# Residual added by an accumulating DMA, and an absolute value by a bit mask, in a gated linear attention followed by a GEGLU layer

## The chip, the cores and the metric

The kernel runs on one core of one Trainium2 chip. The metric is the device time of one execution in microseconds (us). Five engines matter: TensorE (PE: matrix products; its weight loads are listed as PEld), VectorE (DVE), ScalarE (ACT), GpSimd (POOL) and SyncE (SP). DMAs are issued from the queues of SP and of POOL. Each engine works through its own instructions in order; an instruction that waits holds up all behind it on that engine.

## What is computed

Two stages. The first is a linear attention with complex decay over batch 4, 8 heads, 768 steps and head size 48; the second is a GEGLU layer with a gated residual over 3072 tokens of width 384 and an inner width of 1536. In the reference, cut to what matters:

```
scale = min(|a|, 0.999) / (|a| + 1e-6)
S_t   = (a_t * scale) * S_{t-1} + k_t v_t^T        (complex a; S starts at 0)
y_t   = q_t . Re(S_t)
x     = y, all heads side by side: 3072 x 384
g, val = x @ w_gate, x @ w_val
out   = x + sigmoid(x @ w_res) * ((gelu(g) * val) @ w_out)
```

All inputs and the output are float32. The kernel keeps x and the operands of the large products in bfloat16.

## The kernel before, in words

The sequence of each batch is cut into three groups of 256 steps, each of two chunks (c = 0, 1) of 128 steps, so there are 12 groups. The groups are put into seven units: unit 0 has one group, units 1 to 5 have two, unit 6 has one. A chunk of 128 tokens is also the block in which the second stage makes its output.

For each group, phase angles and decay magnitudes come from `a_re` and `a_im`:

- `p1_steps` (lines 179 to 200): logarithm of the magnitude and the ratio that becomes the angle, ACT and DVE in turn (L189, L197 and L198 on DVE); `p1_arctan` makes the angle.
- `cs_l` sums the logarithms within a chunk on PE (L212); `ex` takes the exponentials E and Ei on ACT.
- `cs_t` (L229) sums the angles on PE (L236, L238; L224 and L226 prepare what is carried over from earlier groups) and reduces them to a fraction of a turn on DVE: L243 makes the rounded value r, L244 the difference fg. When the second chunk is done, L246 writes the absolute value of fg beside it, for both chunks at once.
- `p2_sin` (L249) takes two sines on ACT, of the absolute fraction and of the fraction itself: the cosine and sine of the angle, CS.
- `products` multiplies q and k with E and Ei (L309, L314) and with CS (L321). `attention` does the rest: transposes (L346, L349), scores (L356) and their mask (L359), chunk states (L386), and the output y (L394, L396), which ACT writes to the tile x (L399) in bfloat16. The state carried from group to group is G (L370 to L375).
- G needs a decay factor M per row. From unit 3 on M is made from values that lie along a row and must be turned into a column. `turn` (L258 to L267) does this by DMAs on POOL's queue: L262 writes one or two rows (dm) to DRAM, L265 reads them back (m) turned, twice for the two halves. `decay3` multiplies the results on DVE (L282, L283).

The second stage, for each unit: `xt_step` transposes x (L424; copies L428 on ACT and L430 on DVE), `gv_step` makes the gate and value products (L439, L443), Gelu on ACT and their product on DVE (L446), `rp_step` the residual gate (L455), and `op_step` the out-projection of one block (L463). `op_step` then multiplies by the gate on DVE (L466), adds x (L467), and SP stores the block (L469).

The main loop calls `phase_x(u)` and `phase_y(u)` in turn. `phase_x(u)` weaves together the out-projections of unit u - 1, the second half of unit u's attention, the sums, exponentials and sines of unit u + 1, and `p1_steps` and `p1_arctan` of unit u + 2. `phase_y(u)` weaves the gate and value products of unit u, the products of unit u + 1 and the first half of its attention. `weave` gives each step a place between 0 and 1, and the steps are recorded in that order; a scheduler that knows the dependences then sets the order on each engine. ACT's function tables are loaded in a fixed order (logarithm and exponential, then sine, then Gelu), so Gelu work of `phase_y` follows the sines of `phase_x`.

POOL's queue carries, besides the transfers of `turn`, the loads of v (L150) and of the weights, and one-element copies (L171) that hold back the v loads until the k of the same group has landed. SP's queue carries the loads of a, q and k and the stores of the output.

Pools: two buffers for the output block ot, ten for x, four PSUM buffers shared by most products.

## Time and profile before

| what | value |
|---|---|
| median of 8 runs | 329.46 us (326.8 to 331.75) |
| the profiled execution | 327.09 us |
| its span, first to last instruction | 325.3 us |
| TensorE clock granted, mean | 0.946 |
| L246, DVE, 12 times | 947 ns each |
| L467, DVE, 24 times | 550 ns each |
| L466, DVE, 24 times | 546 ns each |
| L198, DVE, 12 times (one input, 128x768 float32) | 555 ns each |
| stores of the output L469, 24 times, 192 KB | 2.2 us from issue to landing |
| v loads on POOL L150, 24 times | 895 ns each to issue |
| L262 and L265 on POOL, 15 and 20 times | 0.51 and 0.70 us each to issue |

How to read it: a group row names line, engine, operation, written and read tiles, shape and count, then busy time and the mean of one in ns, then idle time of the engine before it and what ended that. A row of waits names who waited for whom, the total in us, how often, and the longest. A row of the timeline has start, duration, engine, line, operation and tiles, and in brackets the idle time before it. A row of stretches has start and end, the length, then the busy time of PE, PEld, DVE, ACT and POOL with the number of instructions, then the granted clock as a share, the share of the DMA engines' time and GB/s. A DVE instruction in a timeline can start a little before the one ahead of it ends.

### The profile page before, as it was taken

Reading aid. Unit: us, or ns where it says so; the run is one execution under the profiler, and the core shown is the slowest. Engines: PE = TensorE matmul, PEld = TensorE weight load, DVE = VectorE, ACT = ScalarE, POOL = GpSimd, SP = SyncE. Lnnn points to the kernel's source line nnn. Section 1 sums busy time; section 2 is a strip of 40 time slices with the busy share of each in tenths; the row PEclk is TensorE's granted clock in tenths of the full one; section 3 lists DMA queues with packets and bytes.
Section 4 is the critical chain, followed back from the end, with each engine's and each line's share of the span. In section 5 each row is a group of like instructions: output and inputs, shape, how many; then the busy total and the mean of one; then the engine's idle time right before and its main releaser. Section 6 shows DMA issues by size and latency. Waiting matters only on the chain. (4 is left out here: it accounts for less than half of the span.)

```text
span 325.3 us, 5797 instructions
## 1 busy us (share of the span) xinstructions
PE 269.4 (83%) x2175; PEld 169.9 (52%) x2200; DVE 248.9 (77%) x453; ACT 209.1 (64%) x353; POOL 57.9 (18%) x93
## 2 busy tenths in 40 slices
PE   0337927799876999778997989998989999899995
PEld 0116624577433666444664546564555665455682
DVE  2456768988499995699992999984999948974463
ACT  4539684556997557967468956568765582756150
POOL 1207413022061220243030360000400002000000
PEclk9955676979999999999999999999999999999999
DMA  8999999989999894476360480000110002100101
GB/s 168 204 193 186 167 180 164 189 159 186 195 174 192 182 92 57 78 169 73 70 53 2 89 108 26 0 2 3 50 50 2 2 0 51 48 2 0 71 29 48
DMA packets 134587, 30.23 MB, mean 93 GB/s; under 512 B 126496, under 2 KB 134560, under 8 KB 134560
## 3 DMA queue, kind: packets, MB, share of 16 engines
q1 hardware_dynamic: 103296, 23.60, 36.3%
q0 software_dynamic: 31264, 6.27, 22.7%
q8 instruction: 17, 0.28, 0.3%
q14 instruction: 10, 0.08, 0.1%
HBM read 31.31 MB, written 4.74 MB: 111 GB/s over the span
## 5 line engine op out<-in xcount | busy, mean ns | idle before, releaser
L439 PE MATMUL gp<-xT,wg 128*128 128x512 bf16 (+1 forms) x236 | 62.6, 348 | 7.1 <-DVE xT L430 3.6
L124 ACT ACTIVATE h<-gp 128x512 bf16<-128x512 f32 (+1 forms) x84 | 44.4, 536 | 33.0 <-PE gp L439 30.5
L443 PE MATMUL vp<-xT,wv 128*128 128x512 bf16 (+1 forms) x243 | 62.2, 349 | 0.3
L446 DVE SCALAR_TENSOR_TENSOR h<-h,vp 128x512 bf16<-128x512 bf16 (+1 forms) x84 | 49.6, 603 | 11.9 <-PE vp L443 8.0
L463 PE MATMUL op<-wo,h 128*128 128x384 bf16 x288 | 50.2, 326 | 7.8 <-ACT Ei L124 5.9
L463 PEld LDWEIGHTS <-h 128*128 128x128 bf16 x288 | 27.8, 98 | 28.4 <-issue 11.0
L351 ACT COPY qk<-tp 96x512 bf16<-96x512 bf16 x48 | 27.9, 580 | 21.5 <-PE tp L349 12.9
L359 DVE TENSOR_TENSOR atm<-at,mask 128x512 bf16<-128x512 f32 x48 | 32.9, 685 | 7.2 <-PE at L356 7.0
L439 PEld LDWEIGHTS <-wg 128*128 128x128 bf16 x252 | 23.3, 98 | 20.3 <-issue 8.1
L443 PEld LDWEIGHTS <-wv 128*128 128x128 bf16 x252 | 23.7, 98 | 15.1
L189 DVE TENSOR_TENSOR ai<-s,ai 128x768 f32<-128x768 f32 x12 | 11.1, 955 | 23.7 <-ACT s L124 23.7
L124 ACT ACTIVATE CS<-fg,hpi 128x768 bf16<-128x768 f32 x12 | 11.2, 935 | 26.0 <-DVE fg L246 26.0
L474 ACT ACT_TABLE_LOAD x21 | 26.9, 1283 | 1.1 <-PEq L612 0.7
L346 PE MATMUL tp<-ident,Q 128*96 128x128 bf16 x192 | 19.9, 229 | 7.1 <-DVE Q L321 6.4
L346 PEld LDWEIGHTS <-Q 128*96 128x96 bf16 x192 | 17.0, 129 | 14.8 <-DVE Q L321 9.9
L349 PE MATMUL tp<-ident,K 128*96 128x128 bf16 x192 | 22.1, 234 | 0.0
L150 POOL DMA_DIRECT2D v<-in_v_dram x24 | 21.4, 895 | 3.3 <-DMA v<-in_v_dram 1.3
L236 PE MATMUL cst<-ai,lt0b 128*128 128x384 f32 x24 | 11.5, 565 | 11.8 <-ACT ai L124 11.0
L352 DVE COPY qk<-tp 96x512 bf16<-96x512 bf16 x48 | 19.8, 413 | 1.7 <-ACT qk L351 1.4
L212 PE MATMUL csl<-ar,lt0a 128*128 128x384 f32 x24 | 11.4, 559 | 10.8 <-DMA ar<-in_a_re_dram 10.8
L356 PE MATMUL at<-qk 96*128 96x128 bf16 x192 | 19.7, 226 | 0.1
L394 PEld LDWEIGHTS <-atm 128*128 128x128 bf16 x192 | 12.7, 97 | 13.2 <-DVE atm L359 11.7
(84 smaller groups left out, 514.7 us busy)
## 6 DMA issues: line engine op xcount, KB each, us to landing
ar<-in_a_re_dram SPq DMA_DIRECT2D x24, 192.0 KB, 4.5
ai<-in_a_im_dram SPq DMA_DIRECT2D x24, 192.0 KB, 4.2
q<-in_q_dram SPq DMA_DIRECT2D x24, 192.0 KB, 3.8
k<-in_k_dram SPq DMA_DIRECT2D x24, 192.0 KB, 3.8
out_dram<-ot SPq DMA_DIRECT2D x24, 192.0 KB, 2.2
v<-in_v_dram POOLq DMA_DIRECT2D x24, 96.0 KB, 5.2
wg<-in_moe_w_gate_dram POOLq DMA_DIRECT2D x4, 288.0 KB, 11.3
wv<-in_moe_w_val_dram POOLq DMA_DIRECT2D x4, 288.0 KB, 12.6
```

What stands on the lines that cost most here:

```text
L124: tab(nc.scalar.activation(**kw))
L150: nc.gpsimd.dma_start(out=t[:, c], in_=rows(v, g, c))
L346: nc.tensor.transpose(out=tp[0:DD, j * 128:j * 128 + 128], in_=Q(x), identity=ident)
L349: nc.tensor.transpose(out=tp[0:DD, 512 + j * 128:640 + j * 128], in_=K(x), identity=ident)
L351: nc.scalar.copy(out=qk[0:DD, 0:512], in_=tp[0:DD, 0:512])
L352: nc.vector.tensor_copy(out=qk[0:DD, 512:1024], in_=tp[0:DD, 512:1024])
L359: nc.vector.tensor_tensor(out=atm, in0=at, in1=mask4, op=OP.mult)
L439: nc.tensor.matmul(out=gp, lhsT=wg[:, fi, ffi * 128:(ffi + 1) * 128], rhs=xT[:, fi, :], start=(fi == 0), stop=(fi == KD - 1))
L443: nc.tensor.matmul(out=vp, lhsT=wv[:, fi, ffi * 128:(ffi + 1) * 128], rhs=xT[:, fi, :], start=(fi == 0), stop=(fi == KD - 1))
L446: nc.vector.scalar_tensor_tensor(out=h2[:, ffi, :], in0=h2[:, ffi, :], scalar=0.5, in1=vp, op0=OP.mult, op1=OP.mult)
L463: nc.tensor.matmul(out=ps, lhsT=h2[:, ffi, jj * 128:(jj + 1) * 128], rhs=wo[:, ffi, :], start=(ffi == 0), stop=(ffi == KF - 1))
L474: tab(nc.scalar.preload_act_table_set(nm))
```

## The change

The absolute value in `cs_t` is made by clearing the sign bit of the value read as a 32-bit integer, an operation with one input, where it was the larger of the value and its negative. In `op_step`, for all units but the last, DVE no longer adds x to the block: SP stores the product alone, and POOL's queue then issues a DMA that reads the bfloat16 tile x and adds it to the stored float32 block in DRAM. The dependence between the two is kept by the framework: POOL waits for the store before it issues the second. The blocks of the last unit (two of 24) are made as before.

```diff
         if c == C - 1:
-            nc.vector.scalar_tensor_tensor(out=fg[:, :, 0, :], in0=fg[:, :, 1, :], scalar=-1.0, in1=fg[:, :, 1, :],
-                                           op0=OP.mult, op1=OP.max)
+            nc.vector.tensor_scalar(out=fg[:, :, 0, :].bitcast(mybir.dt.int32), in0=fg[:, :, 1, :].bitcast(mybir.dt.int32),
+                                    scalar1=0x7FFFFFFF, scalar2=None, op0=OP.bitwise_and)
...
         nc.vector.scalar_tensor_tensor(out=ot, in0=T["sg", u][:, jj], scalar=1.0, in1=ps, op0=OP.add, op1=OP.mult)
-        nc.vector.tensor_tensor(out=ot, in0=ot, in1=T["x", token(u, jj)], op=OP.add)
         t0 = token(u, jj) * 128
+        if u == NU - 1:
+            nc.vector.tensor_tensor(out=ot, in0=ot, in1=T["x", token(u, jj)], op=OP.add)
         nc.sync.dma_start(out=out[t0:t0 + 128, :], in_=ot)
+        if u < NU - 1:
+            nc.gpsimd.dma_start(out=out[t0:t0 + 128, :], in_=T["x", token(u, jj)], accum_op=OP.add)
```

In the changed file the accumulating DMA is on line 472, the store on 470 and the remaining addition on 469; the lines up to 466 are where they were.

## Prediction

> **What bounds the kernel now.** I read the share of each engine first, then a table of stretches, then the waits, and last the timelines of VectorE (DVE) and GpSimd (POOL) in one stretch. The profiled execution took 327.09 us; its span is 325.3, so 1.8 us lie around it. It belongs to the faster half of the eight runs (median 329.46). I work in differences and take the sum off the median.

> ```profile
> span 325.3 us, 5797 instructions
> ## 1 busy us (share of the span) xinstructions
> PE 269.4 (83%) x2175; PEld 169.9 (52%) x2200; DVE 248.9 (77%) x453; ACT 209.1 (64%) x353; POOL 57.9 (18%) x93
> ```

> No engine is full. The program alternates between phase_x (decay and angle work, the out-projection) and phase_y (the gate and value matmuls). I cut the span at the ScalarE (ACT) table loads. The next five rows are phase_x of units 1 to 5, which I call S1 to S5; the last row is the phase_y between S3 and S4.

> ```profile
> 83.00:103.60 20.60, 15.21 (x84) 7.80 (x84) 16.29 (x26) 18.53 (x28) 6.94 (x10) 1.00 1.25 184
> 128.40:150.40 22.00, 17.52 (x88) 9.42 (x87) 17.52 (x32) 18.33 (x28) 8.47 (x13) 1.00 0.58 105
> 174.60:196.70 22.10, 18.57 (x92) 10.33 (x92) 17.47 (x34) 18.43 (x29) 8.34 (x13) 1.00 0.51 81
> 221.80:240.60 18.80, 16.54 (x86) 9.41 (x86) 15.04 (x28) 14.79 (x23) 4.78 (x8) 1.00 0.13 34
> 265.60:279.50 13.90, 12.62 (x72) 7.20 (x72) 10.06 (x20) 7.65 (x11) 1.98 (x3) 1.00 0.16 44
> ...
> 196.70:221.80 25.10, 24.44 (x259) 15.44 (x262) 22.70 (x41) 15.25 (x30) 0.00 (x0) 1.00 0.01 1
> ```

> After the length come TensorE (PE), its weight loads, DVE, ACT and POOL. In phase_y PE is busy 24.44 of 25.10 us: PE is the bound there, and a shorter DVE buys next to nothing. In S1 to S5 PE leaves 5.4, 4.5, 3.5, 2.3 and 1.3 us, 17 us together; that is all that this change can win there. Whether DVE holds these stretches is told by the waits:

> ```profile
> ACT CS L124 <- DVE fg L246: 26.0, 12, 5.7
> ...
> DVE M L282 <- DMA m<-dm: 0.9, 1, 0.9
> ```

> Both sines of every group (ACT, 12 pairs) wait for the L246 that the change edits. After the last sine come the Gelu table and phase_y, so phase_y begins when DVE has reached its last L246. The second row matters as much: once DVE waited for the decay factors, which POOL's queue brings. DVE in S4, the start first, then the duration:

> ```profile
> 230.52 0.55 DVE L198 TENSOR_SCALAR ar<-ar 128x768 f32<-128x768 f32 x1
> 230.99 0.55 DVE L467 TENSOR_TENSOR ot<-ot,x 128x384 f32<-128x384 f32 x1
> 231.46 1.08 DVE L243 TENSOR_SCALAR r<-cst 128x384 f32<-128x384 f32 x2
> ...
> 234.25 0.55 DVE L243 TENSOR_SCALAR r<-cst 128x384 f32<-128x384 f32 x1
> 234.75 0.16 DVE L282 TENSOR_TENSOR M<-m 96x8 f32<-96x8 f32 x1
> ...
> 236.63 0.95 DVE L246 SCALAR_TENSOR_TENSOR fg<-fg 128x768 f32<-128x768 f32 x1
> 237.50 0.55 DVE L467 TENSOR_TENSOR ot<-ot,x 128x384 f32<-128x384 f32 x1
> ```

> DVE runs without a break, so what is taken out moves everything behind it. What counts is the distance between starts: 0.47 us for L467 (230.99 to 231.46) and for L198, 0.87 for L246 (236.63 to 237.50).

> POOL in the same stretch; the pair L265 brings the factors that L282 reads at 234.75:

> ```profile
> 229.55 0.48 POOL L262 DMA_DIRECT2D dm<-E  x1 [0.61 <-ACT E L124]
> 230.65 1.50 POOL L265 DMA_DIRECT2D m<-dm  x2 [0.61 <-DMA dm<-Ei]
> 232.14 0.52 POOL L262 DMA_DIRECT2D dm<-ar  x1
> ```

> **The mask.** The twelve L246 become one-input operations of the same 768 elements. Nearest row: L198, also one input, 555 ns against 947 ns. The new one is int32 and steps over 48 of every 96 elements, which no row shows; at worst it costs what L246 costs. [...] So I take L198's pace: 0.87 - 0.47 = 0.40 us each. [...]

> **The residual add.** 22 of 24 L467 go from DVE (22 x 0.47 = 10.3 us of its time); the last two stay, at the end of the program. The store of SP waits for L466 instead, some 1.3 us earlier, with no new queueing in front of it; only its neighbours among the loads shift. In their place POOL gets 22 transfers L472 (96 KB read, 192 KB added in DRAM), each of which waits for its store: 2.2 us median from issue to landing, 1.8 to 4.1. POOL works in order, so all behind it waits too: the v loads, the copies L171, and the decay transfers L262/L265. Issue on POOL: L262 takes 0.51 us for 16 rows and the v loads 0.9 us for 128 x 8 pieces; L472 has 128 rows, nearer the former, so 0.6 (between 0.5 and 0.9). Their time in flight no row shows; a plain store's 2.2 is the lower end, three times that, for reading, adding and writing in turn, the upper; it matters only where a transfer behind it is urgent (S3, S4). Behind the last one lies no work; it is done some 10 us before the end. Tile x is held longer, but its ten buffers come round two units later.

> **Stage by stage**, in the order in which the built program puts the instructions (the scheduler moved some). Savings count up to the last L246.

> - The two stages before S1 hold one and two masks: 0.4 + 0.8. Thereafter PE waits for a chain of ACT work in a part where DMA is 90% busy; between 0 and 1.2, I take half, 0.6.
> - S1: one L467 (0.47), two masks (0.8), one L466 now behind the mask (0.47): 1.7. POOL stands until the store of the first token lands (issued 102.30 behind SP's loads, so about 106); the decay pieces and v loads behind it are needed only from S2 on.
> - S2: three L467 (1.4), two masks (0.8), less an L224 moved ahead and L282 (0.55): 1.65. Its m transfers were issued at 134.3, ahead of the first L472: no new wait.
> - S3: three L467 and two masks: 2.2. But L282 now stands in front of the last L246, and DVE reaches it at 190.04 (before, the L243 in front of it ended its turn at 190.91 + 0.47 = 191.38; less two L467 and one mask, 1.34). Its data come from the second of an L265 pair, issued at 187.26 and 188.13 after the transfers that feed it had come in, as they will again (the L472 ahead of the pair, whose store now goes out at about 181.6, is issued by 185); that transfer takes 3.3 us: 191.5. DVE stands 1.4 us. Left: 0.6.
> - S4: two L467 (0.94), two masks (0.8), less an L224 moved ahead (0.47): 1.25. L282: the L265 pair was issued at 230.65 and 231.40, and landed 3.1 us later by the median, the second at about 234.7: DVE was just in time already. Now POOL has L472 (0.6, in what was idle time) in front of the pair, and an L262 (0.52) between its two: landing at about 235.3. DVE arrives at 234.75 less two L467 and a mask, 1.33, plus an L314 (0.87) that the new order puts in front: 234.3. It stands 1.0 us. Left: 0.2.
> - S5: its L265 pair is ahead of all L472, and lands at 273.9 as before; DVE waited for it already. Only the mask behind it counts: 0.4.
> - From 279.5 on PE does not wait: 0.

> Sum: 0.6 + 1.7 + 1.65 + 0.6 + 0.2 + 0.4 = 5.15 us, against 17 that PE leaves. The profiled execution would take 322.0, the median 329.46 - 5.15 = 324.3.

> **Rivals.**
> - *All of the DVE time counts*: L282 is not held, and what lies behind the last L246 (xT L430, Q L321) counts too. S3 gives 2.0, S4 1.3, S1 to S4 some 0.4 more each: 9 us, 320.5. For it: PE's own waits at the ends of these stages are for xT L430. Against it: L282 stands ahead.
> - *Hidden*: PE's order was rearranged as well (blocks of attention and of gate matmuls change places from S1 on), the mask runs at the old pace (1.75 left), or the early stages give nothing. 326.5 to 331, say 328.
> - *Slower*: the accumulating transfers hold POOL's transfer rings, so that the m transfers issued behind them in S3 and S4 land late and DVE stands at L282. Every us of lateness costs one. The other stages give 4.35; lateness of 2.6 us in each (5.15 in all) takes everything, 5 us in each ends at 334. For it: in S4 the pair follows an L472 at once. Against it: the L265 at 192.23, just behind two v loads of 96 KB, took 2.8 us, no more than alone.

> **Chances.** Likeliest 0.45 (323 to 326.5 us), all counts 0.15, hidden 0.22, slower 0.18. A single measurement tells about 1% from no change, 3.3 us here: faster by more than that is the likeliest and the first rival, 0.60; same 0.22; slower 0.18. Range: from 320.5 (first rival) to 330.5, which leaves out most of the slower one.

> **What would show it.** Right: the new L246 near 0.55 us; ACT's wait for fg below 26 us; L282 waiting about 1.4 us in S3 and 1 us in S4; 22 fewer L467 and no longer S1, S2; phase_y unchanged. Wrong: L246 at 0.95 us; L265 landing over 5 us; an L282 wait of several us; a v load or k load late enough that PE or ACT waits for it.

## The result, and the profile after

| | before | after |
|---|---|---|
| median | 330.51 us (326.02 to 332.11, 32 runs) | 324.03 us (323.23 to 324.88, 11 runs) |
| profiled execution, span | 327.09, 325.3 | 324.58, 322.6 |

The ratio is 0.9874, 95% interval 0.9838 to 0.991. The ratio leaves out those runs of the kernel before that lie over 1.5% above its fastest; they are part of the story below, since the change makes them disappear. The ratio stands for about 4 us. The quotient of the medians is 0.980, that of the two profiled executions 0.992. Three measures of one change differ that much because the runs of the kernel before lie in groups, from 326 to 332 us, and its profile is from the lowest one.

First the rows of the page of the changed kernel that answer to those of before: DVE has 13.9 us and 22 instructions less, POOL 22.8 us and 22 instructions more, PE the same.

```profile
span 322.6 us, 5828 instructions
## 1 busy us (share of the span) xinstructions
PE 269.8 (84%) x2175; PEld 170.3 (53%) x2200; DVE 235.0 (73%) x431; ACT 209.7 (65%) x353; POOL 80.7 (25%) x115
```

Then the same stretches, S1 to S5 and the phase_y between S3 and S4:

```profile
83.10:102.40 19.30, 14.85 (x84) 7.79 (x84) 14.99 (x25) 18.45 (x28) 4.42 (x6) 1.00 1.29 184
127.50:147.90 20.40, 17.03 (x86) 9.19 (x86) 15.39 (x29) 18.35 (x28) 9.59 (x13) 1.00 0.63 128
172.70:194.10 21.40, 18.39 (x90) 10.13 (x90) 16.07 (x31) 18.41 (x29) 11.08 (x16) 1.00 0.60 92
219.20:237.90 18.70, 16.43 (x92) 9.34 (x91) 13.81 (x26) 14.74 (x22) 7.07 (x11) 1.00 0.29 64
262.90:276.10 13.20, 11.90 (x69) 7.05 (x69) 8.18 (x17) 7.67 (x12) 3.87 (x5) 1.00 0.34 63
...
194.10:219.20 25.10, 24.88 (x261) 15.45 (x263) 22.05 (x40) 15.43 (x30) 0.98 (x2) 1.00 0.14 26
```

S1 and S2 are 1.3 and 1.6 us shorter than in the rows of before, S3 and S5 0.7, S4 0.1; phase_y is as long as it was. The two rows of waits: ACT waits 4.9 us less for fg, and DVE stands three times at L282 instead of once, for 2.5 us more.

```profile
ACT CS L124 <- DVE fg L246: 21.1, 10, 5.0
...
DVE M L282 <- DMA m<-dm: 3.4, 3, 1.5
```

DVE in S4, with the mask at 0.46 us from start to start (230.74 to 231.20) and the stand in front of L282:

```profile
230.74 0.55 DVE L246 TENSOR_SCALAR fg<-fg 128x768 int32<-128x768 int32 x1
231.20 0.55 DVE L243 TENSOR_SCALAR r<-cst 128x384 f32<-128x384 f32 x1
232.86 0.16 DVE L282 TENSOR_TENSOR M<-m 96x8 f32<-96x8 f32 x1 [1.11 <-DMA m<-dm]
232.95 0.55 DVE L224 TENSOR_TENSOR P<-ai 128x384 f32<-128x384 f32 x1
```

POOL in S4. The pair L265 that L282 waits for starts at 228.44 and 229.70, with an L472 in front and an L262 between, the order that the prediction read from the built program:

```profile
227.64 0.91 POOL L472 DMA_DIRECT2D out_dram<-x  x1 [0.25 <-DMA dm<-Ei]
228.44 0.88 POOL L265 DMA_DIRECT2D m<-dm  x1
229.22 0.60 POOL L262 DMA_DIRECT2D dm<-ar  x1
229.70 0.87 POOL L265 DMA_DIRECT2D m<-dm  x1
```

### The profile page after: what moved, and what is told of

It is laid out like the page before. It is cut to its first block, busy times and chain, and to the rows that moved or that the text cites. A ratio compares the mean times of both kernels' runs of the same rounds, so it can differ in the third digit from the quotient of the medians.

```text
span 322.6 us, 5828 instructions
## 1 busy us (share of the span) xinstructions
PE 269.8 (84%) x2175; PEld 170.3 (53%) x2200; DVE 235.0 (73%) x431; ACT 209.7 (65%) x353; POOL 80.7 (25%) x115
## 4 chain that ended last, share of the span: by engine, by line
PE 59%; ACT 17%; DVE 11%; DMA 6%; issue 5%; POOL 1%; SPq 0%; DVEq 0%; ACTq 0%; POOLq 0%
PE gp L439 13%; PE vp L443 13%; ACT s L124 6%; PE op L463 5%; PE rp L455 4%; PE tp L346 4%; ACT L477 4%; PE tp L349 4%; PE at L356 3%; PE cst L236 3%; DMA m<-dm 3%; PE csl L212 2%; PE y L394 2%; ACT ar L124 2%; DMA ar<-in_a_re_dram 2%
## 5 line engine op out<-in xcount | busy, mean ns | idle before, releaser
L124 ACT ACTIVATE h<-gp 128x512 bf16<-128x512 f32 (+1 forms) x84 | 44.5, 536 | 38.5 <-PE gp L439 37.9
L439 PE MATMUL gp<-xT,wg 128*128 128x512 bf16 (+1 forms) x241 | 63.4, 352 | 4.4 <-ACT h L124 1.9
L472 POOL DMA_DIRECT2D out_dram<-x x22 | 20.0, 936 | 53.0 <-DMA out_dram<-ot 41.8
L124 ACT ACTIVATE CS<-fg,hpi 128x768 bf16<-128x768 f32 x12 | 11.2, 935 | 21.2 <-DVE fg L246 21.1
L171 POOL COPY landed<-k 1x1 f32<-1x1 f32 x10 | 6.6, 656 | 57.0 <-DMA k<-in_k_dram 57.0
```

The source lines that it names most:

```text
L124: tab(nc.scalar.activation(**kw))
L439: nc.tensor.matmul(out=gp, lhsT=wg[:, fi, ffi * 128:(ffi + 1) * 128], rhs=xT[:, fi, :], start=(fi == 0), stop=(fi == KD - 1))
```

## The experiments

For stage lengths I use the starts of the ACT table loads: S1 to S5 run from the logarithm table to the Gelu table, Y0 to Y5 from there to the next logarithm table. Each set of experiments comes with runs of the kernel before, made on the same chip between its own.

**The two parts alone, and the accumulating DMA alone.** Four kernels, run together; the kernel before had a median of 331.28 us there.

e1, the mask in the kernel before:

```diff
-            nc.vector.scalar_tensor_tensor(out=fg[:, :, 0, :], in0=fg[:, :, 1, :], scalar=-1.0, in1=fg[:, :, 1, :],
-                                           op0=OP.mult, op1=OP.max)
+            nc.vector.tensor_scalar(out=fg[:, :, 0, :].bitcast(mybir.dt.int32), in0=fg[:, :, 1, :].bitcast(mybir.dt.int32),
+                                    scalar1=0x7FFFFFFF, scalar2=None, op0=OP.bitwise_and)
```

> The kernel before with the bit mask alone; the DVE addition of x stays. Order of instructions on DVE as before. Theory (DVE's way to the last L246 sets the end of S1 to S5): each mask ahead of the last one saves 0.40 us: S1 0.8, S2 0.8, S3 0.8, S4 0.4 (DVE waits at L282 for the decay factors, which come no earlier), S5 0.4; sum 3.2, some of it given back in phase_y: ratio 0.990 to 0.994. Rival (the addition that left DVE made the whole gain): 0.998 to 1.002.

Measured: 325.81 us (324.2 to 326.75, 6 runs), ratio 0.985 (0.9815 to 0.9885).

e2, the residual part in the kernel before, L246 as it was:

```diff
-        nc.vector.tensor_tensor(out=ot, in0=ot, in1=T["x", token(u, jj)], op=OP.add)
+        if u == NU - 1:
+            nc.vector.tensor_tensor(out=ot, in0=ot, in1=T["x", token(u, jj)], op=OP.add)
         nc.sync.dma_start(out=out[t0:t0 + 128, :], in_=ot)
+        if u < NU - 1:
+            nc.gpsimd.dma_start(out=out[t0:t0 + 128, :], in_=T["x", token(u, jj)], accum_op=OP.add)
```

> The accumulating DMA alone; L246 as before. Theory: 0.9 us in S1, 0.85 in S2, 0.2 or less in S3, nothing in S4 and S5 since DVE stands at L282: 1.75 us, ratio 0.993 to 0.997. Rival (the 10.3 us that the L467 took on DVE count wherever they were): 0.985 to 0.989, nearly the whole gain of the change.

Measured: 326.52 us (323.82 to 327.55, 6 runs), ratio 0.9854 (0.9812 to 0.9897).

e3, the changed kernel without its accumulating DMA (x is then missing from the output of all units but the last):

```diff
-        if u < NU - 1:
-            nc.gpsimd.dma_start(out=out[t0:t0 + 128, :], in_=T["x", token(u, jj)], accum_op=OP.add)
```

> The changed kernel without the accumulating DMA: x is left out of the output of all units but the last. Theory: the transfers on POOL cost only what they delay L282 in S3 and S4, 0.5 to 1 us together: 0.5 to 1.5 us faster than the changed kernel (ratio to before 0.983 to 0.987, where the changed kernel has 0.987). Rival (POOL's transfers and the traffic of 192 KB reads and writes hold up loads or the decay factors for more): 3 us or more faster than the changed kernel, ratio 0.978 or below.

Measured: 322.28 us (321.57 to 323.1), ratio 0.9742 (0.9708 to 0.9775).

e4, the kernel before with the accumulating DMA besides (x is then added twice):

```diff
         nc.sync.dma_start(out=out[t0:t0 + 128, :], in_=ot)
+        if u < NU - 1:
+            nc.gpsimd.dma_start(out=out[t0:t0 + 128, :], in_=T["x", token(u, jj)], accum_op=OP.add)
```

> The kernel before with all its DVE work, and the accumulating DMA besides (x is added twice for all units but the last): the price of the POOL side alone. Theory: only L282 in S4 comes later, by 0.5 to 1 us; stores are late nowhere: ratio 1.001 to 1.004. Rival (the transfers hold POOL's rings or SP's loads in several stages): 1.010 or more. If the spread of the runs of the kernel before (326 to 332 us, where the changed kernel has 323 to 325) goes with the L467 on DVE, this kernel and the mask alone keep it and the other two lose it.

Measured: 331.0 us (326.92 to 332.75, 14 runs), ratio 0.9952 (0.9903 to 1.0001).

What follows. Each part alone gives a little over half of the stages' gain: S1 to S5 together are 2.5 us shorter than before in e1 and 2.5 in e2, and 4.5 with both (means of all profiles of before and after, below). As times both missed their theory: e1's ratio lies below both of its ranges, e2's in that of its rival. Each alone brought the median down by over 4 us, more than its stages hold; what is beyond them does not come from DVE's path in S1 to S5. The spread missed its forecast too: e4 kept it (326.9 to 332.8 us), but the runs of e1 and of e2 lie within 2.6 and 3.7 us, against 5.7 for the kernel before. e3 puts the price of the accumulating DMA at 1.75 us of the changed kernel's median, a little more than the 0.5 to 1.5 of its theory, though its ratio to before lies where only its rival had it. e4 is inconclusive as a ratio, below the 1.001 that I expected; its profile shows S4 0.5 us and S5 0.1 us longer than any of before and the other stages as they were, and its interval rules out a price of 1% and more.

**Where the price of the DMA lies.** Three kernels on the changed one, run together.

e5, the accumulating DMAs behind the L265 pairs (with 12 buffers for x):

```diff
-            nc.gpsimd.dma_start(out=out[t0:t0 + 128, :], in_=T["x", token(u, jj)], accum_op=OP.add)
+            T.setdefault("late", []).append((t0, T["x", token(u, jj)]))
...
-        phase_x(u)
+        phase_x(u); [tc.add_manual_dep(nc.gpsimd.dma_start(out=out[t0:t0 + 128, :], in_=xt, accum_op=OP.add).ins, T["turned"].ins.name, order, reason="behind the turns") for t0, xt in T.pop("late", [])]
```

> The changed kernel with its 22 accumulating DMAs collected in phase_x and issued behind the pairs of L265 of the same phase (a scheduling edge on GpSimd; the x pool grows from 10 to 12 buffers so that x can wait). TensorE, ScalarE, VectorE and SyncE keep the changed kernel's order; only GpSimd's differs. Leaving the adds out altogether was worth 1.75 us, 0.8 of it in each of the stages S3 and S4. Theory (place in the queue: the adds in front of L262 and L265 hold m up, and VectorE stands at L282): most of it comes back, 322.3 to 323.0 us, 0.995 to 0.998 of the changed kernel, stages S3 and S4 0.5 to 0.8 us shorter, L282's waits down from 3.4 us to 2.5 or less. Rival (presence: what costs is an add being issued or moved while VectorE works, wherever it stands): 323.7 to 324.5 us, S3 and S4 as in the changed kernel, L282's waits shorter all the same.

Measured: 323.72 us (322.6 to 324.4, 6 runs), ratio 0.9845 (0.9808 to 0.9883). S1 to S5 were 17.59, 19.06, 19.42, 16.96 and 11.88 us, with 2.5 us of waits at L282. In e3 they were 17.59, 19.06, 19.34, 16.66 and 12.18, also with 2.5 us. So behind the turns the DMAs cost the stages nothing: the theory of the place in the queue holds for them. As a time it isn't shown: the median lies at the lower edge of the rival's range. It is 0.3 us below the changed kernel's first and 0.8 below its second, and the profiled execution gave 0.6 of its 1.8 us back ahead of S1, where the loads come in.

e6, decay3's products on POOL:

```diff
-        nc.vector.tensor_tensor(out=M[0:DD], in0=m[0:DD, 0], in1=m[0:DD, 1], op=OP.mult)
-        nc.vector.tensor_tensor(out=M[0:DD], in0=M[0:DD], in1=T["m1", g][0:DD, 0], op=OP.mult)
+        nc.gpsimd.tensor_tensor(out=M[0:DD], in0=m[0:DD, 0], in1=m[0:DD, 1], op=OP.mult)
+        nc.gpsimd.tensor_tensor(out=M[0:DD], in0=M[0:DD], in1=T["m1", g][0:DD, 0], op=OP.mult)
```

> The changed kernel with the two small products of decay3 (L282 and L283, 96x8) on GpSimd instead of VectorE, so that VectorE no longer stands in its queue for m; the scheduler then moves other instructions too. Theory (VectorE's 3.4 us at L282 lengthen the stages S3 to S5): 321 to 323 us, S3 and S4 together 1 to 2 us shorter than in the changed kernel. Rival (the wait at L282 is hidden or comes back in the next stage, and GpSimd standing for m holds later adds and loads of v): 323.5 to 325.5 us.

Measured: 330.15 us (328.56 to 331.81, 12 runs), ratio 1.0028 (0.9994 to 1.0061). e7, both edits:

> Both of the above at once: the adds behind the pairs of L265, and decay3's products on GpSimd. If the two costs are different ones (queue place, and VectorE standing) they add up: 320.5 to 322 us, below the changed kernel and below either edit alone by 0.5 us or more. If they are one cost seen twice: the time of the better of the two, within 0.5 us.

Measured: 328.59 us (326.3 to 330.6, 12 runs), ratio 0.9991 (0.9947 to 1.0035). No expectation held for either: the edit costs 5 to 6 us. S2 and S3 are 3.9 and 3.4 us longer in e6. Its POOL timeline in S2:

```profile
137.88 0.20 POOL L282 TENSOR_TENSOR M<-m 96x8 f32<-96x8 f32 x1 [3.45 <-DMA m<-dm]
138.44 0.94 POOL L472 DMA_DIRECT2D out_dram<-x  x1 [0.36 <-issue]
139.07 0.54 POOL L283 TENSOR_TENSOR M<-M,m 96x8 f32<-96x8 f32 x1
```

An L472 lies between the two products, but it is not what costs the time: in e7 nothing lies between them (L282 starts at 137.53, L283 at 137.81), and S2 is 4.8 us longer. In both, POOL stands over 3 us for m, and DVE waits for the second product, because the scheduler, which took M to be ready early, placed G's product L373 ahead of the sums (waits of e6 from 134 to 146 us, then its stretches):

```profile
DVE G L373 <- POOL M L283: 2.0, 1, 2.0
```

```profile
138.00:142.00 4.00, 0.36 (x3) 0.06 (x1) 2.36 (x6) 2.15 (x3) 2.76 (x6) 1.00 0.97 189
142.00:146.00 4.00, 3.43 (x12) 1.70 (x13) 4.00 (x9) 1.78 (x3) 2.33 (x4) 0.57 0.52 115
```

PE was busy for 0.36 of 4 us, and in the next 4 us its granted clock was 0.57. This was the hint for the other half of the story.

**What the groups of runs are.** The kernel before again, three times for a profile:

> The kernel before, unchanged, to have one more profile of it: its runs lie in two groups, about 326.0 to 328.4 us and 330.1 to 332.2 us, and the profile at hand (327.1 us) is of the lower one. If this one is of the upper group, its stages show where the 4.5 us between them lie: by the theory of the matrix clock, in phase_y and the first 60 us, with a lower granted clock in some slices and no longer busy times on VectorE; by its rival, a transfer landing later, in one or two stages alone, at the same clock.

> The kernel before, unchanged, once more for its profile. If it is a run of the upper group (330.1 us and above): by the theory of the clock, TensorE's granted clock is below 1.0 behind the gaps that end at about 64 and 104 us, Y0 and Y1 are 1.3 to 1.7 us longer each, and VectorE's rows are those of the profile at 327.1 us. If of the lower group: clock 1.0 behind the second gap.

> The same once more: an upper run shows phase_y(1) at about 27.7 us with the clock fallen behind the second gap, a lower one 26.0 us with the clock at 1.0.

The executions took 329.14, 331.76 and 329.19 us; with the 327.09 of the first profile the lower group, the upper one and the middle are seen. From S2 on, the stages and the phases from Y2 on are equal within 0.13 us in all four. What differs lies in three places: the time up to S1 (82.97, 82.97, 86.19 and 83.39 us in the order 327.09, 329.14, 331.76, 329.19), S1 itself (19.3 to 20.0), and Y1, which is 26.04 in the first and 27.69, 27.68 and 27.56 in the others. First the execution of 331.76 us, around the start of Y1, then that of 327.09:

```profile
104.00:107.40 3.40, 1.22 (x8) 0.49 (x7) 3.40 (x5) 3.37 (x5) 0.64 (x2) 1.00 1.03 224
...
108.00:111.00 3.00, 3.00 (x19) 1.79 (x18) 2.23 (x5) 1.18 (x2) 0.00 (x0) 0.51 0.94 208
```

```profile
100.90:104.30 3.40, 1.17 (x9) 0.44 (x7) 3.40 (x5) 3.37 (x5) 1.24 (x2) 1.00 0.91 171
104.30:107.30 3.00, 3.00 (x32) 1.98 (x32) 2.97 (x7) 1.85 (x4) 0.00 (x0) 1.00 1.08 244
```

In both, PE is busy for 1.2 of 3.4 us; most of the rest it waits for ACT's Gelu to free the buffer of the next gate product (1.8 us), and 0.4 us for Q from DVE. In the first the clock then falls to 0.51, and in 3 us 19 matmuls start instead of 32; in the second it stays at 1.00. In each of the 14 profiles the granted clock changes only at points that lie whole multiples of 3.41 us apart: in the first of before its stretches last 3.41, 6.83, 10.24 and 20.48 us, and one lasts 256.0. Where these points fall differs from execution to execution: the last fall ahead of S1 runs from 64.95 to 68.36 us there, and from 64.00 to 70.83 in the changed kernel. Laid over the weak stretch, the points cut out an interval in which PE is busy for 1.18, 1.40, 1.56 and 1.57 us in the four profiles whose clock fell there (e10, e11, e1, e8), and for 1.61 and 1.70 us in the two that were spared (the first of before, and e4). So in these six profiles the work in that interval parts those that were hit from those that were spared, with a margin of 0.04 us; that it decides who is hit is my estimate and not shown.

The time up to S1 holds the clock as well. These are the rows of Y0, with the same 225 matmuls, for the executions of 327.09 and 331.76 us, the changed kernel, and e9, which comes below:

```profile
64.13:82.97 18.84, 18.07 (x225) 14.65 (x225) 16.46 (x35) 12.04 (x26) 4.04 (x6) 0.91 1.20 170
66.00:86.19 20.19, 19.25 (x225) 15.60 (x225) 16.24 (x35) 12.14 (x26) 3.87 (x6) 0.83 1.18 170
62.87:83.07 20.20, 19.24 (x225) 15.58 (x225) 16.24 (x35) 12.14 (x26) 3.87 (x6) 0.83 1.26 182
65.69:83.34 17.65, 16.57 (x225) 13.50 (x225) 16.15 (x35) 12.02 (x26) 3.85 (x6) 1.00 1.22 167
```

A mean clock of 1.00, 0.91 and 0.83 is none, 3.4 and 6.8 us at half the clock. Y0 follows it in all 14 profiles: 17.65 us, 18.6 to 19.0, and 20.0 to 20.4. So of the 3.2 us that the execution of 331.76 us loses ahead of S1, 1.35 are the clock in Y0. The other 1.9 lie before Y0; there too the clock came back later, at 56.9 us instead of 54.7, but which of the two is the cause is not shown.

Back to the weak stretch at the start of Y1. In the changed kernel it has twice the PE work:

```profile
101.00:104.40 3.40, 2.29 (x24) 1.40 (x23) 3.40 (x5) 2.96 (x5) 0.00 (x0) 1.00 1.03 227
104.40:108.00 3.60, 3.54 (x37) 2.24 (x36) 3.40 (x9) 1.79 (x4) 1.95 (x3) 1.00 1.11 226
```

In e1, where the mask alone is changed, PE is busy for 1.58 of the 3.4 us, the clock fell, and Y1 took 27.68. In e2, without L467, it is busy for 1.98, the clock held, and Y1 took 26.40. So it is the residual part that closes the gap, together with the order of PE that comes with it (in Y1, e2's differs from that of before and e1's does not), and not the mask.

Can the gap be closed by itself? e9 is the kernel before with 12 matmuls in this gap whose result nobody reads, and 7 more in a like gap at about 62 us, just before Y0:

```diff
+    def fill(n, last):
+        yd = psY.tile([128, DM], FP, tag="y", padded_shape=[128, 512], name="yd")
+        for _ in range(n):
+            f = nc.tensor.matmul(out=yd, lhsT=ident, rhs=wg[:, 0, 0:DM], start=True, stop=True)
+            tc.add_manual_dep(f.ins, last.ins.name, order, reason="fill")
...
+                if (g, c, hg) == (1, 0, 0):
+                    fill(7, last)
...
+        if (u, ffi) == (1, 1):
+            fill(12, last)
```

> The kernel before with 19 more matmuls whose result nobody reads (128x384 bf16, into the idle y buffer): 7 behind the first transposes of Q of group 1, where TensorE stands from about 61.4 to 62.8 us, and 12 around those of group 3, where it stands from 102.4 to 104.3 us. VectorE, ScalarE, GpSimd and SyncE keep the order of the kernel before. In its profiles TensorE is busy for only 0.35 of the 3.4 us that end with each of these gaps, and in the changed kernel nowhere for under 0.48. In a profile at 329.1 us and in that of the mask alone the granted clock falls to 0.5 just behind the second gap, and phase_y(1) is 1.65 us longer. Theory (the upper group of runs is the kernel with its clock fallen behind these gaps): with them filled the upper group is gone: all or nearly all runs below 328.5 us, median 325.5 to 327.5 us, 0.984 to 0.990 of the kernel before, though TensorE has 3 us more to do. Rival (the groups have another cause): both groups stay, median 329.5 to 331.5 us, 0.998 to 1.003.

Measured: 328.99 us (327.3 to 330.94, 12 runs), ratio 0.9994 (0.9953 to 1.0035); its runs of before had a median of 330.34, and 8 of the 17 lay above 331. Its profile has the gap filled and the clock held:

```profile
100.90:104.30 3.40, 3.22 (x21) 1.80 (x20) 3.40 (x6) 3.30 (x4) 1.11 (x2) 1.00 0.90 168
104.30:107.30 3.00, 2.70 (x26) 1.68 (x26) 2.97 (x6) 1.85 (x4) 0.00 (x0) 1.00 1.09 245
```

Y1 took 26.03 us, and Y0 17.65. So in this profile the clock held in both places, at 1.00, where the execution of 331.76 us has a mean of 0.83 in Y0 and 0.51 behind the gap in Y1, and the runs above 331 us are gone; but the median came down by 1.35 us, not by 3 to 5, the ratio shows no gain, and neither expectation met it. The one profile lost again what it won: Y0 began at 65.69 us, 1.2 later than the mean of before, a turn in S5 landed late (POOL's wait for dm 3.0 us there, 1.3 before; S5 1.4 us longer), and the part behind Y5 was 0.6 us longer. What keeps its runs above 327 us is open. The changed kernel once more:

> The changed kernel, unchanged, for more runs and a second profile. Theory: the upper group of the kernel before is its clock, fallen behind the gap at 101 to 104 us; the change has closed that gap (TensorE never under 0.46 busy over 3.4 us after 70 us), so no run falls: phase_y(1) 26.4 us again, the stages S1 to S5 within 0.1 us of the first profile of the changed kernel except S1, where the loads still come in, all runs between 322.5 and 325.5 us, 0.979 to 0.985 of the kernel before. Rival (the first eleven runs were lucky): some runs at 326 us and above, with phase_y(1) at 27.7 us or more.

Measured: 324.49 us (323.29 to 325.57, 6 runs), ratio 0.9848 (0.9793 to 0.9903). Y1 was 26.39 us with the clock at 1.00. Of its 17 runs in all, none is above 325.6 us. S3 and S5 missed my 0.1 us: 19.89 and 12.37 against 20.12 and 11.94.

## Why the prediction was right, and where it wasn't

The forecast level, 324.3 us, met the measured 324.03, and the stages that carry most of the forecast are right; that the totals met so closely is in part luck. All profiled executions together, four of before and two of after, in us:

| stretch | before | after | change | predicted |
|---|---|---|---|---|
| up to S1 | 83.88 | 83.48 | -0.40 | -0.6 |
| S1 | 19.59 | 17.95 | -1.64 | -1.7 |
| S2 | 20.70 | 19.07 | -1.63 | -1.65 |
| S3 | 20.80 | 20.00 | -0.80 | -0.6 |
| S4 | 17.48 | 17.52 | +0.04 | -0.2 |
| S5 | 12.60 | 12.16 | -0.44 | -0.4 |
| Y1 | 27.24 | 26.40 | -0.84 | 0 |
| Y2 to Y5 and the end | 125.23 | 126.52 | +1.29 | 0 |
| span | 327.52 | 323.10 | -4.42 | -5.15 |

The five stages are the prediction's strong side: 4.47 us against 4.55, each within 0.25. Its "From 279.5 on PE does not wait: 0" and the zero for the other phase_y were wrong twice, with opposite signs, and the right total owes something to that. So does the row up to S1: Y0 begins 1.24 us earlier, which is about the whole 1.2 of the three masks ahead of it (but its start varies by 2.6 us among the four of before), and then lasts 0.84 us longer, because both profiles of after have 6.8 us at half the clock there and only two of the four of before. And the level was taken off 329.46 us, the median of eight runs; that of all 32 is 330.51, and the medians fell by 6.5 us, not by 5.15.

- *The mask.* Predicted 0.40 us each by the row of L198; that the int32 form would keep that row's pace was an estimate, which no run of before shows. Measured 0.41 (0.87 to 0.46 us from start to start). The int32 read with a step takes 550 ns in the median. The 0.95 that was kept as the worst case came once, and beside issues of POOL. DVE and POOL in S3:

```profile
190.07 0.98 DVE L246 TENSOR_SCALAR fg<-fg 128x768 int32<-128x768 int32 x1
190.98 0.34 DVE L430 COPY xT<-tpx 128x384 bf16<-128x384 bf16 x1
```

```profile
188.87 1.80 POOL L150 DMA_DIRECT2D v<-in_v_dram  x2 [0.41 <-issue]
190.65 0.96 POOL L472 DMA_DIRECT2D out_dram<-x  x1
191.24 1.71 POOL L265 DMA_DIRECT2D m<-dm  x2
```

  DVE paid 0.43 us, and POOL next to nothing (0.96 us for this L472, 0.94 in the mean). The L472 is not the cause by itself. In e1, which has none, a mask beside two loads of v took 709 ns, and in e7 one beside a load of v and an L265 took 1002. In e12 the same mask beside the same L472 took its usual time:

```profile
190.91 0.55 DVE L246 TENSOR_SCALAR fg<-fg 128x768 int32<-128x768 int32 x1
...
190.88 0.97 POOL L472 DMA_DIRECT2D out_dram<-x  x1
```

  In the seven profiles with the new mask, 35 of 84 overlap an issue of a DMA by POOL, and only these three took over 0.65 us. Whether POOL's issues stand behind the three is open; beside such an issue the other 32 took 0.65 us at most.
- *The residual add, on DVE.* L467 at its pitch of 0.47 us, stage by stage: S1 and S2 are right to 0.06 us, where nothing else stands in the way.
- *L472 on POOL.* Predicted 0.6 us to issue, in bounds of 0.5 to 0.9; it takes 936 ns, just above the upper one. The nearer row was that of the v loads (0.9), not that of L262. In flight it takes 3.8 us, between the bounds 2.2 and 6.6. The group row of the page:

```profile
L472 POOL DMA_DIRECT2D out_dram<-x x22 | 20.0, 936 | 53.0 <-DMA out_dram<-ot 41.8
```

  POOL stands 41.8 us for stores. What the standing and the issues cost together is the price in the next point, under 2 us: little of what lies behind them is urgent.
- *L282 in S3 and S4.* Predicted stands of 1.4 and 1.0 us; 0.79 and 1.11 measured. In S4 the mechanism is shown to the instruction; in S3 the pair L265 was issued at 184.98 and 185.75 us, 0.3 to 0.4 us earlier in its stage than the prediction had it. e3 and e5 give the price of the queue: 1.9 and 1.8 us over S1 to S5.
- *phase_y.* In Y2 to Y5 the time given back goes with the order of PE's instructions and nothing else that I tried. After, e3, e5 and e12 have the same order of PE and the same Y2 to Y5 within 0.02 us (26.08, 26.38, 26.32, 23.18); e4, with the order of before, has that of before (25.55, 26.35, 26.26, 22.73). In e1 PE's order differs from that of before only in Y5, and of these four that phase alone is longer, by 0.52. The prediction saw that "PE's order was rearranged as well" and put it under a rival without a price; it was a term of the sum, 1.05 us over Y2 to Y5, with 0.36 more in Y1. The 0.25 us after Y5 are not explained.
- *The clock.* The prediction read 1.00 in its stretches, from a profile in which it was, and put no price on the clock. In three of four profiles of before it fell in Y1, at 1.5 to 1.65 us each. The change closes that gap: this is the -0.84 of Y1 (a gain of 1.2 on average, less the 0.36). It is also part of why the median fell by 6.5 us, more than the 4.4 of the profiles: of the 70 runs of before in the four sets of experiments, 47 are above 329.7 us, and only one of the four profiles is from there (331.76), with this loss and the 3.2 us ahead of S1, of which 1.35 are the clock in Y0.

The rivals: "all counts" overrated the stages; "hidden" named the rearranged order rightly but with too high a price; "slower" is out, since m lands 3.2 us after its issue by the median, as before (3.15), and e4 bounds the price of the DMAs in the old order.

## What to carry to other kernels

A sum over stages, read from the wait that ends each one, held to a few tenths here, also where two queues meet; what it leaves out is what the scheduler does to the order of the engine that is the bound, so price that order too. Before trusting a profile as the base of a sum, see whether its time is where most runs are; if it isn't, look for a stretch in which TensorE does little for some 3 us (here 1.2 to 1.6 of 3.4) and read the granted clock behind it. Here one fall cost 1.5 to 1.65 us in the executions that had it; but filling the gaps alone (e9) showed no gain in the ratio, so price it by several executions. A bulk issue in front of a small, urgent transfer on the same queue cost 1.8 us of the stages here (e5), and moving the consumer onto that queue's engine (e6), with the new order that the scheduler made of it, was worse than letting it stand.
